# Two attention-and-MLP layers on one core: the last two chunks of a second product taken tile by tile, and four smaller moves of loads and steps around it

## The chip, the cores and the metric

The kernel runs on one core of one Trainium2 chip. The metric is the device time of one execution in microseconds (us). The kernel before was run three times: 2491.26, 2492.43 and 2493.83 us, median 2492.43. One more execution was profiled, and its records are the trace that is read here.

## The reference

The input is x of 2048 rows by D = 576 columns in f32. Two equal layers follow one another, each an attention and an MLP on a normalised x, with a residual sum after each:

```python
x = x + _A_ref(_layernorm(x), A_wqkv, A_w_phi, A_wo)      # twice in turn
x = x + _B_ref(_layernorm(x), B_w1, B_b1, B_w2, B_b2)

# _A_ref: 32 heads of width 18
q, k, v = split(x @ wqkv)
phi(t)  = concat(softmax(t @ w_phi), softmax(-(t @ w_phi)))
o       = phi(q) @ (phi(k)^T v) / (phi(q) @ sum(phi(k)) + 1e-6)
return o @ wo

# _B_ref: F = 4608
return relu(x @ w1 + b1)**2 @ w2 + b2
```

The attention is linear: the sums `phi(k)^T v` of all 2048 rows must be there before the first row of `o`, so each layer has a point at which every block waits for every other one.

## The kernel before

The rows lie in four blocks of 512 (`TB`), each of four tiles of 128 rows (`NT`); F lies in 36 chunks of 128 (`NF`). Operands of the products are split into a high and a low part, and each product is three matrix products (high by high, high by low, low by high). TensorE (PE) works through one fixed list of 15108 matmuls; VectorE (DVE), ScalarE (ACT) and GpSimd (POOL) normalise, split and add, and nearly all DMAs are issued from SyncE's queue (SP), in the order in which the program wrote them. No engine changes the order of its own list, so an instruction that waits holds up all that stands behind it on its engine.

The program is written with Python generators: `weave`, `lagged`, `pipeline`, `chained` and `paced` set by a table of costs in which order the steps of two generators are written, and `tc.issue_after(ins)` makes what stands under it come behind `ins` in the written order.

The stages of a layer, with the names of tiles that the trace shows (`a_2`, `m_3` and so on are block numbers; layer 0 takes the blocks in the order 3, 2, 0, 1, layer 1 in the order 1, 0, 3, 2):

- A barrier finishes the keys of the last block and then runs the attention's output stage for the first block (`g_out` with `pause`, L895 on). Tiles there begin with `t0` in layer 0 and `t1` in layer 1: `t0fQ2e` and `t0fQ3e` are the exponentials of the queries of row tiles 2 and 3, `t0opt` their transposes, `t0oo0h`/`t0oo1l` the two halves of wo in high and low parts, stored to memory as `wsoh`/`wsol` for later blocks, `t0ox` the rows of x, `t0opo` the product with wo, `t0onn`/`t0onp`/`t0onh` the normalised rows, their transposes and these in high part.
- `g_mlp` does the MLP of the first block (`m_3` in layer 0), woven with the attention of the second (`a_2`), and then that of the second block (`m_2`), woven with the attention of the two last (`a_0`, `a_1`). For each chunk `first` loads w1 (`r1`) and w2 (`r2`, L1093) and splits them (ACT takes the high part of w2 at L1100 as `m_2s`), `hidden` is the first product, `square` the activation, and `second` the second product. The first two chunks' `hidden` are done in halves of 256 columns, the second half after the last transposes of the normalised rows (`last`, L1065 to L1074, called through `rest` at L1164).
- `g_pair` does the MLP of the two last blocks together (tiles `m_p...`). `products` forms the first product of both by a Strassen-like scheme and the second product of the one block; `seconds` forms the second product of the other, chunks 36 to 71, with row sums in the PSUM tiles `m_pach` and `m_pacacc`; `last_rows` (L1478 to L1499) ends each of the two: the last chunk, four transposes back (`m_ppy<-ident,m_pyt`), the sum with the residual rows `m_px` (the first 448 columns, `:R`, at L1496 and the last 128 at L1492), and the stores.
- In layer 0 the `seconds` are woven at a rate of 0.85 with `back_keys`: the norms, keys and values of layer 1 for three blocks (tiles `n_3`, `w_3v`, `k_0K3`). Its norm is `g_norm` with `fine` (L542): `begin` takes the statistics of a row tile (`n_3s`, `n_3m`) and the factor `n_3d`, which POOL forms; `scale` writes `n_3n` and `n_3e`; transposes (`n_3p`) and splits (`n_3h`, `n_3l`) follow. After the `seconds` come the values and keys of the last block, with a norm of its own (`n_last`).

Around the change, these lists of the program set the order: in `g_out`, `pieces()` loads or forms the halves of wo and `keep_split` stores them; `between` holds twelve small steps between the two parts of the paused block; in the main loop `next(back)` sets how many steps of `back_keys` are written before the `seconds` begin.

Of the kernel before, what the change touches and what calls it, by code (L numbers as in the profile page):

```python
# [15 lines left out]
NT = TB // P  # L16
# [5 lines left out]
def layers_kernel(  # L22
# [18 lines left out]
    nc = tc.nc  # L41
# [410 lines left out]
    def g_norm(x_of, dst, name, then=None, fine=False):  # L452
# [86 lines left out]
            else:  # L539
                split_main(i // 3 * 2 + i % 3, pts.pop(i))  # L540

        yield from pipeline(NT, (start, apart), (2.0, 1.6))  # L542
        yield from pipeline(3 * NT // 2, (cross, split), (0.3, 0.9))

    def spill(b, x):
# [312 lines left out]
    def g_out(layer, b, ph, dst, name, parts=1, pause=None, behind=None, norm=None, mid=None, costs=(None, None)):  # L858
# [88 lines left out]
        if pause:  # L947
            product, total, factors, rescale = pause()
            with tc.issue_after(dense["scaled0"].ins):
                product(2, 0)  # L950
                total(2, 0)
        pair = pieces() if behind or "o" in kept else None
        if pair:
            keep_split("o", pair)
        if pause and not late:
            late_products()
        xs_of = []
        yield

        def between(pts):  # L960
            steps = [lambda: product(3, 0), lambda: total(2, 1), lambda: factors(2), lambda: rescale(2, 1),
                     lambda: total(3, 0), lambda: total(3, 1), lambda: factors(3), lambda: rescale(3, 1),
                     lambda: o_add(xs_of[0], pts[0], 0), lambda: o_add(xs_of[1], pts[1], 0),
                     lambda: rescale(2, 0), lambda: rescale(3, 0)]
            for step in steps:
                step()
                yield

        for part in range(parts):
            if pause and part:  # L970
                xs_of += [rows_in(t) for t in range(2)]
                pts = [o_product(t, half) for half in range(2) for t in range(2)]
                with tc.issue_after(dense["part"].ins):
                    drain(chained(between(pts), every=True))
            for i, _ in enumerate(lagged(2 * NG, lambda i: turn(part, i), lambda i, f: times(part, i, f), parts)):
                if pause and part and i in (1, 2):
                    with tc.issue_after(dense["turned"].ins):
                        o_add(xs_of[i - 1], pts[1 + i], 1)
                yield costs[0]
# [84 lines left out]

        def last():  # L1065
            spare.update(tags=[f"acc{i}" for i in range(NC)], i=NC + 1)
            pts = [main[0](t, xns[t]) for t in (2, 3)]
            pts.append(rest[0](1))
            spare["tags"] = []
            yield  # L1070
            main[1](2, pts[0])
            main[1](3, pts[1])
            rest[1](1, pts[2])
            yield  # L1074

        dense["rest"] = last()
# [2 lines left out]
    def g_mlp(layer, b, x, after, name, rest=None, then=None):  # L1079
# [277 lines left out]
    def g_pair(layer, blocks, x, after, name):  # L1357
# [119 lines left out]

        def last_rows(b):  # L1478
            f = (b + 1) * NF - 1
            features(f, range(3))  # L1480
            yt = sb.tile([P, TB], F32, tag="hr", name=f"{name}yt{b}", bufs=2)
            nc.scalar.activation(yt, accs[b][KC], AF.Copy)
            by_rows(f, range(2), range(3))
            pt = ps_w.tile([P, TB], F32, tag="w", name=f"{name}py{b}")
            p3 = pt.rearrange("p (t d) -> p t d", d=P)
            for t in range(NT):
                nc.tensor.transpose(p3[:, t], yt[:, t * P : (t + 1) * P], ident)
            xs_ = after if b else []
            for t in range(NT):
                xr = sb.tile([P, D], F32, tag="x", name=f"{name}x{b}{t}", bufs=5)  # L1490
                nc.sync.dma_start(xr, xm[blocks[b]][t])
                nc.vector.tensor_add(xr[:, R:], p3[:, t], xr[:, R:])  # L1492
                xs_.append(xr)
            by_rows(f, range(2, NT), range(3))
            for t, xr in enumerate(xs_):
                dense["added"] = nc.vector.tensor_add(xr[:, :R], accs[b][t][:, :R], xr[:, :R])  # L1496
                at = blocks[b] * TB + t * P
                nc.sync.dma_start(out[at : at + P] if layer else xs[blocks[b]][t], xr)
            del high[f], wide[f]  # L1499

        def keep_high(f, r):
            nc.scalar.activation(r, r, AF.Relu)
# [78 lines left out]
        def seconds():  # L1581
            accs[1] = [ps_a.tile([P, TB], F32, tag=tag, name=f"{name}ac{tag}") for tag in ("h", "acc0", "acc1", "acc2", "acc3")]
            for f in range(NF, NF + 3):
                load_wide(f)
                load_high(f)
            for f in range(NF, 2 * NF - 1):
                if f + 3 < 2 * NF:
                    load_wide(f + 3)
                    load_high(f + 3)
                for t in range(NT):  # L1590
                    by_rows(f, [t], range(3))
                    yield
                features(f, range(3))
                del high[f], wide[f]
                yield
# [125 lines left out]
    for layer in range(2):  # L1721
# [145 lines left out]
```

## Time and profile before

| | |
|---|---|
| runs, us | 2491.26, 2492.43, 2493.83; median 2492.43 |
| profiled execution, its own time, us | 2491.15 |
| span of its records, us | 2489.2 |
| TensorE, busy and share of the span | 2463.1 us, 99% |
| VectorE | 1535.0 us, 62% |
| ScalarE | 1263.0 us, 51% |
| GpSimd | 956.7 us, 38% |
| granted TensorE clock, mean of the span | 0.999 |

Times in the rows of the trace are microseconds from the start of the span: first the start, then the busy time, then the engine (SPq is the queue that SyncE issues from), the line, the operation, the tile written and the tiles read, and a count where several equal rows stand in one. In square brackets stands how long the engine was idle just before, and what ended that. The view of waits has the engine, tile and line that waited, what released it, and then the sum in us, the count and the longest one.

### The profile page before, as it was taken

How to read it: one execution, taken by the hardware profiler on the slowest of the kernel's cores; microseconds unless marked ns; L12 is line 12 of the kernel's file. 1: busy time of each engine (PE TensorE's matmuls, PEld its weight loads, DVE VectorE, ACT ScalarE, POOL GpSimd, SP SyncE). 2: the span in 40 equal slices, each digit the busy share in tenths (PEclk: the TensorE clock that was granted, in tenths of full speed). 3: DMA queues.
4: the chain of work that ended last, by engine and by line, in shares of the span. 5: the costliest groups of instructions: out<-in, count | busy, mean ns of one | idle time of the engine just before them, and what ended most of it. 6: DMA issues, size and time to landing. Idle time of an engine off the chain costs nothing. (4 is left out here: it accounts for less than half of the span.)

```text
span 2489.2 us, 41471 instructions
## 1 busy us (share of the span) xinstructions
PE 2463.1 (99%) x15108; PEld 2169.4 (87%) x15108; DVE 1535.0 (62%) x2507; ACT 1263.0 (51%) x2243; POOL 956.7 (38%) x1101
## 2 busy tenths in 40 slices
PE   8999999999999999999999999999999999999999
PEld 8998888889888888888999988888888888888888
DVE  7778938454756655545756787584557665454454
ACT  4344545443546766664443445554445466666543
POOL 4445303212335565541433442132122355565322
PEclk9999999999999999999999999999999999999999
DMA  9124533346434433338754144334473444333363
GB/s 332 60 71 146 169 105 94 103 156 224 131 120 134 146 104 105 110 100 287 250 196 144 54 169 116 103 99 117 153 243 96 125 136 139 115 104 112 108 200 127
DMA packets 248892, 348.67 MB, mean 140 GB/s; under 512 B 30127, under 2 KB 155951, under 8 KB 246127
## 3 DMA queue, kind: packets, MB, share of 16 engines
q1 hardware_dynamic: 247428, 344.66, 44.0%
q8 instruction: 118, 1.93, 0.3%
q10 hardware_dynamic: 1258, 1.37, 0.2%
q14 instruction: 88, 0.71, 0.1%
HBM read 280.93 MB, written 65.00 MB: 139 GB/s over the span
## 5 line engine op out<-in xcount | busy, mean ns | idle before, releaser
L1428 POOL TENSOR_TENSOR m_ps<-m_pr,m_ps 128x128 fp32r<-128x128 f32 x144 | 118.2, 821 | 310.9 <-ACT m_ps L1426 248.7
L1427 DVE TENSOR_TENSOR m_ps<-m_pr,m_ps 128x448 fp32r<-128x448 f32 x144 | 97.9, 680 | 166.1 <-ACT m_ps L1426 162.6
L1470 PE MATMUL m_pacc<-m_ps,m_phb 128*128 128x448 f32 x864 | 188.5, 366 | 0.0
L1470 PEld LDWEIGHTS m_pacc<-m_ps,m_phb 128*128 128x128 f32 x864 | 162.1, 188 | 18.2
L1426 ACT ACTIVATE m_ps<-m_pr 128x576 fp32r<-128x576 f32 x144 | 98.4, 683 | 128.1 <-issue 71.5
L1470 PE MATMUL m_pacacc<-m_ps,m_phc 128*128 128x448 f32 x648 | 150.3, 368 | 0.7 <-DVE m_px L1496 0.7
L1470 PEld LDWEIGHTS m_pacacc<-m_ps,m_phc 128*128 128x128 f32 x648 | 119.2, 188 | 10.0 <-DVE m_px L1496 1.0
L1148 PE MATMUL m_0acc<-m_0s,m_0hb 128*128 128x448 f32 x432 | 100.2, 366 | 0.0
L1148 PE MATMUL m_2acc<-m_2s,m_2hb 128*128 128x448 f32 x432 | 100.2, 366 | 0.0
L1148 PE MATMUL m_3acc<-m_3s,m_3hb 128*128 128x448 f32 x432 | 99.7, 365 | 0.0
L1148 PE MATMUL m_1acc<-m_1s,m_1hb 128*128 128x448 f32 x432 | 99.7, 365 | 0.0
L1121 PE MATMUL m_3ph<-t0onh,m_3h 128*128 128x512 f32 (+1 forms) x380 | 97.6, 382 | 0.6 <-ACT t0onh L488 0.5
L1121 PE MATMUL m_1ph<-t1onh,m_1h 128*128 128x512 f32 (+1 forms) x380 | 97.5, 382 | 0.6 <-ACT t1onh L488 0.5
L1121 PE MATMUL m_2ph<-a_2nh,m_2h 128*128 128x512 f32 (+1 forms) x380 | 97.7, 384 | 0.0
L1121 PE MATMUL m_0ph<-a_0nh,m_0h 128*128 128x512 f32 (+1 forms) x380 | 97.6, 384 | 0.0
L1148 PEld LDWEIGHTS m_2acc<-m_2s,m_2hb 128*128 128x128 f32 x432 | 80.9, 188 | 10.6 <-ACT m_2hb L1129 0.2
L1148 PEld LDWEIGHTS m_0acc<-m_0s,m_0hb 128*128 128x128 f32 x432 | 80.9, 188 | 10.6 <-ACT m_0hb L1129 0.2
L1148 PEld LDWEIGHTS m_1acc<-m_1s,m_1hb 128*128 128x128 f32 x432 | 81.1, 188 | 10.3
L1148 PEld LDWEIGHTS m_3acc<-m_3s,m_3hb 128*128 128x128 f32 x432 | 81.1, 188 | 10.3
L1106 POOL TENSOR_TENSOR m_3s<-m_3r,m_3s 128x128 fp32r<-128x128 f32 x36 | 24.6, 684 | 161.6 <-ACT m_3s L1100 148.1
L1106 POOL TENSOR_TENSOR m_1s<-m_1r,m_1s 128x128 fp32r<-128x128 f32 x36 | 24.2, 673 | 162.2 <-ACT m_1s L1100 154.8
L1106 POOL TENSOR_TENSOR m_0s<-m_0r,m_0s 128x128 fp32r<-128x128 f32 x36 | 28.1, 779 | 138.8 <-ACT m_0s L1100 131.1
(2439 smaller groups left out, 7341.3 us busy)
## 6 DMA issues: line engine op xcount, KB each, us to landing
m_pr<-in_B_w SPq DMA_DIRECT2D x144, 288.0 KB
m_pr<-in_B_w SPq DMA_DIRECT2D x72, 256.0 KB
hd<-m_pu SPq DMA_DIRECT2D x72, 256.0 KB
m_pg<-hd SPq DMA_DIRECT2D x72, 256.0 KB
m_3r<-in_B_w SPq DMA_DIRECT2D x36, 288.0 KB
m_2r<-in_B_w SPq DMA_DIRECT2D x36, 288.0 KB
m_1r<-in_B_w SPq DMA_DIRECT2D x36, 288.0 KB
m_0r<-in_B_w SPq DMA_DIRECT2D x36, 288.0 KB
```

The lines of the kernel that those rows point to most:

```text
L1106: nc.gpsimd.tensor_sub(s2[:, D + R : 2 * D], r2[:, R:], s2[:, R:D].bitcast(F32))
L1121: dense["hidden"] = nc.tensor.matmul(ph[:, cols], a, m, start=(k == 0), stop=(k == len(ops) - 1))
L1148: nc.tensor.matmul(acc[t][:, :R], a[:, rows], m, start=(f == 0 and k == 0), stop=(f == NF - 1 and k == 2))
L1426: nc.scalar.activation(s2[:, :D], r2, AF.Copy)
L1427: nc.vector.tensor_sub(s2[:, D : D + R], r2[:, :R], s2[:, :R].bitcast(F32))
L1428: nc.gpsimd.tensor_sub(s2[:, D + R : 2 * D], r2[:, R:], s2[:, R:D].bitcast(F32))
L1470: nc.tensor.matmul(accs[b][t][:, :R], a[:, rows], m, start=(g == 0 and k == 0), stop=(g == NF - 1 and k == 2))
```

## The change

The arithmetic, the tiles' sizes and the number of matmuls stay. Six places are written in another order:

1. `g_norm`, fine path: the statistics of row tile t+1 are written before the scaling of row tile t; before, `pipeline` wrote both steps in its own order.
2. `g_out`: the first two loads of x rows stand ahead of the stores of the split wo. In `between`, `product(3, 0)` goes from first to fourth. Blocks without `behind` load their halves of wo at turn `NG` of the loop, where they did so after it.
3. `last` and `g_mlp`: the transposes of row tile 2 and its splits are written after the first half chunk of `hidden`, those of row tile 3 and the rest after the second; before, all stood after the second.
4. `last_rows` of the second block (`b = 1`): chunks `NF - 2` and `NF - 1` are taken together. The last 128 columns' sums (`features`) of both come first, then rows 0 and 1 with both chunks each, the transposes, and rows 2 and 3. Each row's two sums and its store follow one another. `seconds` ends one chunk earlier.
5. `last_rows` of the first block (`b = 0`): all four sums of the 448 columns first, then for each row the sum of the 128 columns and its store.
6. Main loop: one step of `back_keys` is written before the last pair ends, and one after the `added` of `last_rows`, where there were two and four.

```diff
@@ g_norm
-        yield from pipeline(NT, (start, apart), (2.0, 1.6))
+        start(0)
+        yield 2.0
+        for t in range(NT):
+            if t + 1 < NT:
+                start(t + 1)
+                yield 2.0
+            apart(t)
+            yield 1.6
@@ g_out
-        pair = pieces() if behind or "o" in kept else None
-        if pair:
-            keep_split("o", pair)
+        pair = pieces() if behind else None
         if pause and not late:
             late_products()
         xs_of = []
+        if pause:
+            xs_of += [rows_in(t) for t in range(2)]
+            keep_split("o", pair)
         yield
...
-            steps = [lambda: product(3, 0), lambda: total(2, 1), lambda: factors(2), lambda: rescale(2, 1),
+            steps = [lambda: total(2, 1), lambda: factors(2), lambda: rescale(2, 1), lambda: product(3, 0),
...
-                xs_of += [rows_in(t) for t in range(2)]
...
+                if not behind and i == NG:
+                    pair = pieces()
@@ last
-            pts = [main[0](t, xns[t]) for t in (2, 3)]
-            pts.append(rest[0](1))
+            pt = main[0](2, xns[2])
             spare["tags"] = []
-            yield
-            main[1](2, pts[0])
-            main[1](3, pts[1])
-            rest[1](1, pts[2])
+            main[1](2, pt)
+            yield
+            spare.update(tags=[f"acc{i}" for i in range(NC)], i=NC + 2)
+            pt, pr = main[0](3, xns[3]), rest[0](1)
+            spare["tags"] = []
+            main[1](3, pt)
+            rest[1](1, pr)
             yield
@@ g_mlp
-        if rest:
-            with tc.issue_after(dense["hidden"].ins):
-                drain(rest)
+            if rest:
+                with tc.issue_after(dense["hidden"].ins):
+                    next(rest)
@@ g_pair, last_rows
-            features(f, range(3))
+            fs = (f - 1, f) if b else (f,)
+
+            def rows_of(ts):
+                for t in ts:
+                    for f in fs:
+                        by_rows(f, [t], range(3))
+
+            for f in fs:
+                features(f, range(3))
...
-            by_rows(f, range(2), range(3))
+            rows_of(range(2))
...
-                nc.vector.tensor_add(xr[:, R:], p3[:, t], xr[:, R:])
+                if b:
+                    nc.vector.tensor_add(xr[:, R:], p3[:, t], xr[:, R:])
                 xs_.append(xr)
-            by_rows(f, range(2, NT), range(3))
+            rows_of(range(2, NT))
             for t, xr in enumerate(xs_):
                 dense["added"] = nc.vector.tensor_add(xr[:, :R], accs[b][t][:, :R], xr[:, :R])
+            for t, xr in enumerate(xs_):
+                if not b:
+                    with tc.issue_after(dense["added"].ins):
+                        nc.vector.tensor_add(xr[:, R:], p3[:, t], xr[:, R:])
                 at = blocks[b] * TB + t * P
                 nc.sync.dma_start(out[at : at + P] if layer else xs[blocks[b]][t], xr)
...
-            for f in range(NF, 2 * NF - 1):
+            for f in range(NF, 2 * NF - 2):
@@ main loop
-                    for _ in range(2):
-                        next(back, None)
+                    next(back, None)
         with tc.issue_after(dense["added"].ins):
-            for _ in range(4):
-                next(back, None)
+            next(back, None)
         weave(seconds, back, 0.85)
```

Three places show how the instructions move on their engines. The numbers behind the names tell tiles of one name apart.

The first is SyncE's queue in layer 0 where the paused block stores its split wo. Before:

```order
L406 DMA wsol<-t0oo0l 126x1152
L406 DMA wsol<-t0oo0l 72x288
L406 DMA wsol<-t0oo1l 126x1152
L406 DMA wsol<-t0oo1l 72x288
L922 DMA t0ox_3119<-in_A_x 128x576
L922 DMA t0ox_3121<-in_A_x 128x576
```

And now:

```order
L406 DMA wsol<-t0oo0l 126x1152
L929 DMA t0ox_3006<-in_A_x 128x576
L929 DMA t0ox_3008<-in_A_x 128x576
L406 DMA wsol<-t0oo0l 72x288
L406 DMA wsol<-t0oo1l 126x1152
L406 DMA wsol<-t0oo1l 72x288
```

The two loads of x rows have passed three stores, two of them of the low half `t0oo1l`.

The second is SyncE's queue in layer 0 at the step from the MLP of block 3 to that of block 2. `a_0o1h` and `a_0o1l` are loads of wo's second half for block 0, `xs` the stores of block 3's rows, `m_2r_2` and `m_2r_3` the loads of w2 for chunks 2 and 3. Before:

```order
L987 DMA xm_3_96<-a_2x_5675 128x576
L406 DMA a_0o1h<-wsoh 126x1152
L406 DMA a_0o1h<-wsoh 72x288
L406 DMA a_0o1l<-wsol 126x1152
L1204 DMA xs_0_81<-m_3x_5979 128x576
L1204 DMA xs_1_82<-m_3x_5981 128x576
L1204 DMA xs_2_83<-m_3x_5983 128x576
L1204 DMA xs_3_84<-m_3x_5985 128x576
L406 DMA a_0o1l<-wsol 72x288
L1093 DMA m_2r_2_6197<-in_B_w 128x576
L1093 DMA m_2r_3_6211<-in_B_w 128x576
```

And now:

```order
L996 DMA xm_3_96<-a_2x_5675 128x576
L1104 DMA m_2r_2_6185<-in_B_w 128x576
L406 DMA a_0o1h<-wsoh 126x1152
L1215 DMA xs_0_81<-m_3x_5979 128x576
L1215 DMA xs_1_82<-m_3x_5981 128x576
L1215 DMA xs_2_83<-m_3x_5983 128x576
L1215 DMA xs_3_84<-m_3x_5985 128x576
L1104 DMA m_2r_3_6199<-in_B_w 128x576
L406 DMA a_0o1h<-wsoh 72x288
L406 DMA a_0o1l<-wsol 126x1152
L406 DMA a_0o1l<-wsol 72x288
```

The load `m_2r_2` stands ahead of the four row stores now, and the loads of `a_0o1` partly behind them. On the four compute engines nothing moves at this place, and the step in layer 1 moves alike.

The third is VectorE in layer 0 where `products` ends and `seconds` begins. `m_ps_36` and `m_phc` are the split operands of chunk 36, the first of the `seconds`. Before:

```order
L438 BN_STATS n_3s_11924<-x_3_0_11922 128x6 x2
L441 BN_AGGR n_3m_11925<-n_3s_11924 128x2
L469 TENSOR_SCALAR n_3n_11932<-x_3_0_11922,n_3m_11925,n_3d_11926 128x512
L470 TENSOR_SCALAR n_3e<-x_3_0_11922,n_3m_11925,n_3d_11926 128x128
L1496 TENSOR_TENSOR m_px_11951<-m_pacc_9173,m_px_11951 128x448
L1496 TENSOR_TENSOR m_px_11954<-m_pacc_9174,m_px_11954 128x448
L1492 TENSOR_TENSOR m_px_11951<-m_ppy_11946,m_px_11951 128x128
L1492 TENSOR_TENSOR m_px_11954<-m_ppy_11946,m_px_11954 128x128
L1492 TENSOR_TENSOR m_px_11957<-m_ppy_11946,m_px_11957 128x128
L1492 TENSOR_TENSOR m_px_11960<-m_ppy_11946,m_px_11960 128x128
L1496 TENSOR_TENSOR m_px_11957<-m_pacc_9175,m_px_11957 128x448
L1496 TENSOR_TENSOR m_px_11960<-m_pacc_9176,m_px_11960 128x448
```

And now:

```order
L438 BN_STATS n_3s_11924<-x_3_0_11922 128x6 x2
L441 BN_AGGR n_3m_11925<-n_3s_11924 128x2
L1438 TENSOR_TENSOR m_ps_36_11991<-m_pr_36_11989,m_ps_36_11991 128x448
L1540 TENSOR_TENSOR m_phc_11997<-m_pg_11995,m_phc_11997 128x512
L1516 TENSOR_TENSOR m_px_11948<-m_pacc_9173,m_px_11948 128x448
L1516 TENSOR_TENSOR m_px_11950<-m_pacc_9174,m_px_11950 128x448
L1516 TENSOR_TENSOR m_px_11952<-m_pacc_9175,m_px_11952 128x448
L1516 TENSOR_TENSOR m_px_11954<-m_pacc_9176,m_px_11954 128x448
L1520 TENSOR_TENSOR m_px_11948<-m_ppy_11943,m_px_11948 128x128
L1520 TENSOR_TENSOR m_px_11950<-m_ppy_11943,m_px_11950 128x128
L1520 TENSOR_TENSOR m_px_11952<-m_ppy_11943,m_px_11952 128x128
L1520 TENSOR_TENSOR m_px_11954<-m_ppy_11943,m_px_11954 128x128
```

The split of chunk 36 stood behind all of these rows and now stands ahead of the residual sums; the scaling of the first row tile (`n_3n`, `n_3e`) now comes after the operands of chunks 38, 40 and 41. On TensorE the transposes `n_3p` of that norm begin in chunk 39, where they began in chunk 37, and the three chunks before run without other work between.

More of the change, by code (lines that the diff above doesn't have):

```diff
@@ L1491, in last_rows @@
                 nc.sync.dma_start(xr, xm[blocks[b]][t])
-                nc.vector.tensor_add(xr[:, R:], p3[:, t], xr[:, R:])
+                if b:
+                    nc.vector.tensor_add(xr[:, R:], p3[:, t], xr[:, R:])
                 xs_.append(xr)
-            by_rows(f, range(2, NT), range(3))
+            rows_of(range(2, NT))
             for t, xr in enumerate(xs_):
                 dense["added"] = nc.vector.tensor_add(xr[:, :R], accs[b][t][:, :R], xr[:, :R])
+            for t, xr in enumerate(xs_):
+                if not b:
+                    with tc.issue_after(dense["added"].ins):
+                        nc.vector.tensor_add(xr[:, R:], p3[:, t], xr[:, R:])
                 at = blocks[b] * TB + t * P
                 nc.sync.dma_start(out[at : at + P] if layer else xs[blocks[b]][t], xr)
-            del high[f], wide[f]
+            for f in fs:
+                del high[f], wide[f]
         def keep_high(f, r):
```

## The prediction

> **What bounds the kernel now.** I read the page's busy times first, then the view of TensorE's (PE) waits, then the lists of rows around each wait that the change can reach.
>
> ```profile
> PE 2463.1 (99%) x15108; PEld 2169.4 (87%) x15108; DVE 1535.0 (62%) x2507; ACT 1263.0 (51%) x2243; POOL 956.7 (38%) x1101
> ```
>
> PE is busy for 99% of the span and the change leaves it the same 15108 matmuls, so all that can be won lies in PE's idle time, 2489.2 − 2463.1 = 26.1 us, part of which is the start before the first product and the end after the last. The waits within reach are few and single:
>
> ```profile
> PE t0opt L888 <- DVE t0fQ2e L805: 3.1, 1, 3.1
> ...
> PE n_3p L494 <- DVE n_3l L489: 1.9, 1, 1.9
> PE a_3pn L904 <- DVE a_3fl L891: 1.8, 1, 1.8
> ...
> PE a_0pn L904 <- DVE a_0fl L891: 1.2, 1, 1.2
> ...
> PE m_1ph L1121 <- ACT t1onh L488: 0.5, 1, 0.5
> PE m_3ph L1121 <- ACT t0onh L488: 0.5, 1, 0.5
> ```
>
> Each of these six occurs once, 9.0 us in all; two more, 1.52 together, stand in part C. Since PE's list is the bound, a microsecond of wait removed from it is worth up to a microsecond, and work on the other engines is free as long as PE does not wait for it. That is the rule by which I cost each part.
>
> **Part A: the x rows ahead of the stores of split wo (layer 0).**
>
> ```profile
> 204.20 1.05 SPq L406 DMA_DIRECT2D wsol<-t0oo0l  x2
> ...
> 207.67 3.96 POOL L384 TENSOR_TENSOR t0oo1l<-t0oo1r,t0oo1h 126x1152 fp32r<-126x1152 f32 x2
> ...
> 209.00 1.98 DVE L828 TENSOR_TENSOR t0fm<-t0fQ3e,zb 128x576 f32<-128x576 f32 x1
> ...
> 212.04 1.78 SPq L922 DMA_DIRECT2D t0ox<-in_A_x  x4
> ...
> 215.00 0.23 DVE L800 TENSOR_TENSOR t0fQ3r<-t0fQ3r,t0fu 128x64 f32<-128x64 f32 x1
> ...
> 216.16 0.46 DVE L939 TENSOR_TENSOR t0ox<-t0opo,t0ox 128x288 f32<-128x288 f32 x1 [0.94 <-DMA t0ox<-in_A_x]
> ...
> 218.09 0.75 DVE L805 TENSOR_TENSOR t0fQ2e<-t0fQ2e,t0fQ2r 128x576 f32<-128x576 f32 x1
> ...
> 218.98 0.41 PE L888 MATMUL t0opt<-ident,t0fQ2e 128*126 128x128 f32 x2 [3.07 <-DVE t0fQ2e L805]
> ```
>
> PE names VectorE (DVE) as what it waits for, but DVE itself stood idle for 0.94 us until a DMA landed. The load was issued at 212.04, because SyncE's queue (SP) held a store of `t0oo1l`, which GpSimd (POOL) finished at 207.67 + 3.96 = 211.63. The change puts two loads behind the first store of `t0oo0l`, so they are issued near 204.20 + 0.5 = 204.7. They landed 216.16 − 212.04 = 4.1 us after issue; now that is about 208.8. The sums then start when DVE's own chain ends, 215.00 + 0.23 = 215.2; two sums of 0.46 and the rescaling of 0.75 end at 216.9, and PE starts 218.98 − 218.84 = 0.14 later, near 217.05. Gain 218.98 − 217.05 = **1.9 us**. At most the whole 3.07 goes. At least 1.9 − 1.2 = 0.7 does: the product of 1.98 at 209.00 has 576 columns like the rescaling of 0.75 but ran beside POOL's 3.96 us, and the steps of DVE's chain now come in another order there, so that some other sum may be held up the same 1.2 us in its place or beside it. The Trainium skill (SBUF — State Buffer, SBUF: two separate sides) states that DVE sums with two operands in SBUF and GpSimd's instructions that read SBUF take one port pair by an exclusive lock for a whole instruction. The row at 209.00 agrees with it: 1.98 is just one of POOL's two subtractions (3.96/2); by the lock a second sum caught there would take up to 1.98 more, and part A would be about nothing.
>
> **Part B: w2 of chunk 2 ahead of the row stores (both layers).**
>
> ```profile
> 516.70 2.60 SPq L1204 DMA_DIRECT2D xs<-m_3x  x4
> ...
> 520.24 1.07 SPq L1093 DMA_DIRECT2D m_2r<-in_B_w  x2
> ...
> 524.17 0.40 PE L1139 MATMUL m_2acc<-m_2hb,m_2s 128*128 128x512 f32 x1
> ...
> 525.97 0.69 ACT L1100 ACTIVATE m_2s<-m_2r 128x576 fp32r<-128x576 f32 x1 [2.10 <-DMA m_2r<-in_B_w]
> 526.56 1.06 ACT L890 ACTIVATE a_0fh<-a_0pt 126x512 fp32r<-126x512 f32 x2
> ...
> 527.97 0.50 PE L904 MATMUL a_0pn<-a_0fh,kbh 126*126 126x512 f32 x1 [1.23 <-DVE a_0fl L891]
> ```
>
> The chain is again a DMA seen through two engines: the load is issued at 520.24, ScalarE (ACT) waits 2.10 us for it with `a_0fh` queued behind, DVE makes `a_0fl` from that, and PE starts 527.97 − 525.97 = 2.00 us after ACT did. PE would have been free at 527.97 − 1.23 = 526.74. Now the load goes ahead of the stores that began at 516.70, at least 3.5 us earlier. ACT's next limit is the buffer of `m_2s`, which chunk 0's second product leaves when its last matmul ends, 524.17 + 0.40 = 524.57. ACT then runs from 524.6, PE could start at 526.6, and that is before 526.74: the whole 1.23 goes.
>
> ```profile
> 1748.03 0.91 SPq L1093 DMA_DIRECT2D m_0r<-in_B_w  x2
> ...
> 1754.50 0.68 ACT L1100 ACTIVATE m_0s<-m_0r 128x576 fp32r<-128x576 f32 x1 [2.66 <-DMA m_0r<-in_B_w]
> ...
> 1756.49 0.50 PE L904 MATMUL a_3pn<-a_3fh,kbh 126*126 126x512 f32 x1 [1.79 <-DVE a_3fl L891]
> ```
>
> Layer 1 has the same shape: PE 1.99 us behind ACT, free at 1754.70; ACT needs to start at 1752.7, 1.8 us earlier than now, and it has been idle for 2.66. Gain **1.23 + 1.79 = 3.0 us**, bounds 0 (the load still late) and 3.0. What is delayed in turn are the loads of `a_0o1` behind the stores, by the four stores' 2.60 us and one load; they are wanted by the output product only after all of block 0's attention numerators, so I take nothing for them.
>
> **Part C: start of the seconds in layer 0.**
>
> ```profile
> 1139.60 2.41 SPq L1498 DMA_DIRECT2D xs<-m_px  x4
> ...
> 1140.75 0.47 PE L1470 MATMUL m_pacacc<-m_ps,m_phc 128*128 128x448 f32 x1 [0.67 <-DVE m_px L1496]
> ...
> 1142.41 1.13 SPq L1742 DMA_DIRECT2D x<-xs  x2
> ...
> 1142.87 0.47 PE L1470 MATMUL m_pach<-m_ps,m_phc 128*128 128x448 f32 x1 [0.85 <-DVE m_ps L1427]
> ...
> 1148.77 0.55 DVE L469 TENSOR_SCALAR n_3n<-x,n_3m,n_3d 128x512 f32<-128x512 f32 x1 [1.00 <-POOL n_3d L443]
> ...
> 1151.54 0.67 DVE L469 TENSOR_SCALAR n_3n<-x,n_3m,n_3d 128x512 f32<-128x512 f32 x1 [1.00 <-POOL n_3d L443]
> ...
> 1152.38 1.28 DVE L489 TENSOR_TENSOR n_3l<-n_3p,n_3h 128x512 fp32r<-128x512 f32 x2
> ...
> 1153.12 0.44 PE L494 MATMUL n_3p<-ident,n_3e 128*128 128x128 f32 x2 [1.90 <-DVE n_3l L489]
> ```
>
> In the queue of DVE before, the normalisation and all residual sums stood ahead of chunk 36's operands, so PE waited 0.67 and 0.85. Now chunk 36's split comes first and PE runs chunks 36 to 38 with nothing between: 1.52 go. The 1.90 at 1153.12 is a wait for `n_3l` behind DVE steps that twice stood idle 1.00 us for POOL's `n_3d` (ahead of 1148.77 and of 1151.54). With the next tile's statistics written first, most of those 2 × 1.00 is covered by the other work that the look-ahead puts there, and this wait shrinks; but the transposes now also come in a tighter group, with two PSUM tiles to turn over, and I leave 1.0 of it. Gain 1.52 + 0.90 = **2.4 us**; at most 0.67 + 0.85 + 1.90 = 3.42, at least 0 (all of it comes back as waits for the norm three chunks later).
>
> **Part D: the later start of the back work, end of layer 0.** Four steps fewer are written ahead of the seconds, so the chain of layer 1's keys ends later. Its last softmax meets this:
>
> ```profile
> 1344.28 0.62 DVE L1496 TENSOR_TENSOR m_px<-m_pach,m_px 128x448 f32<-128x448 f32 x1 [5.30 <-PE m_pach L1470]
> ...
> 1355.22 0.60 ACT L488 ACTIVATE n_lasth<-n_lastp 128x512 fp32r<-128x512 f32 x1 [0.88 <-PE n_lastp L480]
> ```
>
> DVE waits 5.30 us for PE there, and the next norm's split waits for PE too (0.88), not PE for it. Three chunks of a pace of 0.85 make the softmax some 5 us later, which that idle time takes up. Cost **0**; if the cover fails by 1 us, PE loses that 1 us at the next norm.
>
> **Part E: the end of the program.**
>
> ```profile
> 2483.68 1.99 SPq L1498 DMA_DIRECT2D out<-m_px  x4
> ...
> 2484.16 1.15 DVE L1496 TENSOR_TENSOR m_px<-m_pacacc,m_px 128x448 f32<-128x448 f32 x2
> ...
> 2484.50:2485.50 1.00, 0.00 (x0) 0.00 (x0) 0.81 (x2) 0.00 (x0) 0.00 (x0) 1.00 0.98 376
> ...
> 2487.50:2489.20 1.70, 0.00 (x0) 0.00 (x0) 0.00 (x0) 0.00 (x0) 0.00 (x0) 0.50 0.04 14
> ```
>
> The last sum ends at 2484.16 + 1.15 = 2485.3; the four stores (4 × 128 × 576 × 4 bytes = 1.18 MB) fill the DMA engines from 2484.5 at 376 GB/s, 3.1 us, to 2487.6. So the end is set by the stores' bytes after a late first issue. Now six matmuls of the chunk before stand behind rows 0 and 1 and the transposes; at 0.2 us each (2463.1 us for 15108 is 0.16, and these are wide ones) the first two stores go about 1.1 us ahead of 2483.68; the last row's sum still follows the last matmul and its store is issued near 2485.1. It starts 2484.5 − 2483.7 = 0.8 to 1.0 later and takes 0.78, to 2486.9. Gain **0.8 us**, bounds 0.2 and 1.2. The Trainium skill (DMA: Bandwidth & Descriptors, Anatomy of one DMA — SWDGE (gpsimd) path) fits a fixed 2.0 us beside the bytes of one transfer, on GpSimd's path; by that figure, an estimate for SyncE's, the last store would complete at 2485.1 + 2.0 + 0.78 = 2487.9 and this term would be about 0.2. The windows show the first bytes within a microsecond of the issue and little after 2487.6, so less than that here.
>
> **Part F: transposes between the half chunks (both layers).**
>
> ```profile
> 238.09 0.49 DVE L469 TENSOR_SCALAR t0onn<-t0ox,t0onm,t0ond 128x512 f32<-128x512 f32 x1
> ...
> 241.72 1.68 PE L1121 MATMUL m_3ph<-t0onh,m_3h 128*128 128x256 f32 x9 [0.52 <-ACT t0onh L488]
> ```
>
> The wait of 0.52 is for the splits of tiles 2 and 3 done at once; with tile 2 earlier it shrinks to some 0.3. But tile 2's transposes now stand half a chunk earlier, at about 238.2, and its scaling on DVE ends at 238.58: 0.4 of new wait. Loss **0.2 us** in each layer, 0.4 in all, bounds a loss of 1.0 and a gain of 0.3.
>
> **Sum.** 1.9 + 3.0 + 2.4 + 0 + 0.8 − 0.4 = 7.7 us. The profiled execution took 2491.15 by its own time, so 2483.45; the median of the runs is 2492.43 − 2491.15 = 1.28 above it, so I forecast **2484.7 us**. About 0.2% (5 us) is what a measurement of this kernel can tell from no change.
>
> **Rivals.**
> 1. *Part C comes back as waits.* The norm's transposes are denser and its rows are loaded behind the four stores. For it: only two PSUM tiles turn over; against: the two idle stretches of 1.00 vanish. Then the sum is 7.7 − 2.4 = 5.3, or less with a new wait of 2: 2487.1 to 2489.
> 2. *Part B doesn't come.* The margin is thin, 526.74 − 526.6 = 0.14 us, and if the landing rather than the buffer still ends ACT's wait, the 3.0 stay. For it: SP is backed up at both places; against: 3.5 us of lead for 1.4 needed. The sum is 4.7: 2487.7, within 0.2%.
> 3. *Slower: x rows late at the start of the seconds.* `x_3_1` to `x_3_3` were issued partly before and now all behind the stores of 1139.60, near 1142.8. DVE stands in order, so a late row stops the operands of later chunks too, and PE with them. At part A's 4.1 us from issue to landing they come at about 1147; by its list DVE comes to the first of them after the residual sums and six splits for chunks 38 to 41, whose operands wait on PE's pace, at about 1147 to 1148. Each microsecond beyond costs PE up to one; it decides when the landing slips by more than 7.7 us, past 1155. With 4 us more than that, 2496.4. For it: the in-order queue; against: a slip twice the usual latency.
> 4. *The edits move waits but remove none*: PE stays at the same total because each place hands its wait on to the next in-order queue (A to DVE's lock, B to ACT's buffer, C to the norm); only E remains, 2491.6.
>
> **How the numbers follow.** Forecast 0.60, rival 1 0.14, rival 2 0.10, rival 3 0.09, rival 4 0.07. The likeliest case's own range is 2482.0 to 2487.0 (A 0.7 to 3.07, C 1.5 to 3.42, E and F by their bounds, not all at one end). With rivals 1, 2 and 4 the range is 2481.0 to 2491.5, which leaves out rival 3 and some of the tails. Faster by over 0.2% (below 2487.4): the forecast 0.60 and a little of rivals 1 and 2, 0.64. Slower: 0.09, rounded to 0.10. Within: the rest, 0.26.
>
> **What would show it.** A: no DMA as what ended DVE's idle time before `t0ox`, and PE's wait for `t0fQ2e` near 1. B: no wait at `a_0pn` and `a_3pn`, the load of `m_2r` no longer behind `xs`. C: no wait of PE at the first three chunks of the seconds, 1.0 or less at the later `n_3p`. E: last bytes about 2.4 us after the last matmul rather than 3.2. F: a wait of about 0.4 at tile 2's `t0onp`. The forecast is wrong if PE shows a new single wait over 2 us in layer 0's seconds or at `n_last`, or if the DVE chain ahead of `t0fQ2e` ends later than 215.2 by more than a microsecond.

## The result, and the profile after

The changed kernel takes 2487.36 us (median of 12 runs, 2483.86 to 2490.75), the kernel before 2491.66 in twelve runs beside it (2488.80 to 2495.03). The ratio is 0.9981 with a 95% interval of 0.9973 to 0.9989: 0.19% faster, or 4.7 us of 2491.7 with 2.7 to 6.7 as bounds. The forecast was 2484.7. The execution that was profiled took 2485.37, so it is one of the faster ones.

The page and the view of TensorE's waits of the changed kernel:

```profile
span 2483.7 us, 41469 instructions
PE 2463.2 (99%) x15108; PEld 2169.5 (87%) x15108; DVE 1533.9 (62%) x2507; ACT 1262.1 (51%) x2243; POOL 959.3 (39%) x1101
```

```profile
PE n_3p L480 <- DVE n_3n L469: 2.7, 1, 2.7
...
PE t0opt L895 <- DVE t0fQ2e L812: 1.2, 1, 1.2
...
PE m_1ph L1132 <- ACT t1onh L488: 0.5, 1, 0.5
PE m_3ph L1132 <- ACT t0onh L488: 0.5, 1, 0.5
```

The waits `a_0pn` (1.2) and `a_3pn` (1.8) are gone, `t0opt` fell from 3.1 to 1.2, and one new wait of 2.7 stands at `n_3p`, at the start of the seconds. To see what each place is worth, each matmul's start in one trace was set against the start of the same matmul in the other; the median difference over a quiet stretch behind each place gives the lead over the kernel before there. The steps of that lead in the two profiled executions are:

| place | forecast gain, us | lead gained, us |
|---|---|---|
| A, x rows ahead of the stores of wo | 1.9 | 2.9 |
| F, transposes between half chunks, both layers | −0.4 | −0.3 and −0.1 |
| B, w2 ahead of the row stores, layer 0 / layer 1 | 1.2 / 1.8 | 1.3 / 1.9 |
| C, start of the seconds (with D) | 2.4 | −1.2 |
| E, end of the program | 0.8 | 0.8 |
| sum | 7.7 | 5.3 |

The spans differ by 5.5 us (2489.2 against 2483.7); small drifts between the places make up the rest. One warning on such sums: over the first 190 us, where none of the kernels below differs, the profiled executions took from 0.9 us less to 1.9 us more than that of the kernel before, so in what follows a place is always read against the lead just ahead of it.

### The profile page after: what moved, and what is told of

It reads as the page before. It is cut to its first block, busy times and chain, and to the rows that moved or that the text cites. A ratio compares the mean times of both kernels' runs of the same rounds, so it can differ in the third digit from the quotient of the medians.

```text
span 2483.7 us, 41469 instructions
## 1 busy us (share of the span) xinstructions
PE 2463.2 (99%) x15108; PEld 2169.5 (87%) x15108; DVE 1533.9 (62%) x2507; ACT 1262.1 (51%) x2243; POOL 959.3 (39%) x1101
## 4 chain that ended last, share of the span: by engine, by line
PE 94%; DVE 3%; DMA 1%; ACT 1%; issue 1%; POOL 0%; SPq 0%; ACTq 0%; DVEq 0%; POOLq 0%
PE m_ppx L1449 9%; PE m_pacc L1481 7%; PE m_pacacc L1481 5%; PE m_ppy L1449 5%; PE m_1ph L1132 5%; PE m_3ph L1132 5%; PE m_0ph L1132 5%; PE m_2ph L1132 5%; PE m_2acc L1159 4%; PE m_0acc L1159 4%; PE m_1acc L1159 3%; PE m_3acc L1159 3%; PE m_ppz L1449 2%; PE m_pacc L1471 2%; PE m_pacacc L1471 2%; PE m_pach L1481 2%
## 5 line engine op out<-in xcount | busy, mean ns | idle before, releaser
L1132 PEld LDWEIGHTS m_3ph<-t0onh,m_3h 128*128 128x128 f32 x380 | 68.8, 188 | 14.0 <-ACT t0onh L488 0.7
```

The costliest lines, as they stand in the source:

```text
L1132: dense["hidden"] = nc.tensor.matmul(ph[:, cols], a, m, start=(k == 0), stop=(k == len(ops) - 1))
```

## The experiments

Profiles show single places to about 0.1 us, timed runs show totals to about 2.5 us; both are given. Ratios are to the kernel before on the same chip.

### Is the new wait a matter of buffers, of a backlog, or of the look-ahead?

The timeline of the changed kernel at the new wait (start, busy time, engine, line, operation, tiles; idle time and its releaser in brackets):

```profile
1136.33 2.88 SPq L1522 DMA_DIRECT2D xs<-m_px  x4
1143.72 1.71 SPq L1767 DMA_DIRECT2D x<-xs  x3
...
1143.60 0.68 DVE L1540 TENSOR_TENSOR m_phc<-m_pg,m_phc 128x512 fp32r<-128x512 f32 x1
1146.59 0.82 DVE L438 BATCH_NORM_STATS2 n_3s<-x 128x6 f32<-128x288 f32 x2 [2.32 <-DMA x<-xs]
...
1148.12 1.12 PE L480 MATMUL n_3p<-ident,n_3n 128*128 128x128 f32 x4 [2.67 <-DVE n_3n L469]
```

VectorE was through with the operands of chunk 41 at 1144.3 and then waited 2.32 us for a row of x, with the scaling of the first tile behind it, and TensorE behind that. The row's load was issued only at 1143.72, 4.5 us after the fourth store. SyncE had been waiting until 1143.68 for the first residual store to land: five buffers hold rows of x, and with the look-ahead the first row is still in use, so the second needs the buffer of a residual row. That store had been issued at 1136.33 and took 7.3 us; in the kernel before the x load that stood behind the same store went 2.8 us after its issue (1139.60 to 1142.41). Most of the bytes were through earlier than that, as the DMA share and GB/s at the end of these two rows show (1.01 and 371, then 0.39 and 153):

```profile
1136.00:1140.00 4.00, 4.00 (x21) 3.62 (x20) 2.03 (x7) 0.73 (x2) 0.47 (x1) 1.00 1.01 371
1140.00:1144.00 4.00, 4.00 (x21) 3.60 (x21) 2.63 (x4) 2.30 (x4) 1.58 (x2) 1.00 0.39 153
```

The last section shows what the store's landing still lacked.

**Six buffers**, wherever the rows' tag stands:

```diff
-                x = sb.tile([P, D], F32, tag="x", name=f"x1_{b}_{t}", bufs=5)
+                x = sb.tile([P, D], F32, tag="x", name=f"x1_{b}_{t}", bufs=6)
```

> The changed kernel with six instead of five buffers for rows of x. Ring theory: the 2.67 us wait of TensorE at the first n_3p (1148.12) exists because the load of x_3_1 needs the buffer of a residual row until that row's store has landed (SyncE waits for xs<-m_px until 1143.68). With a sixth buffer the load is issued right behind the four stores near 1139.3, the wait falls to 0.5 or less, the granted clock stays 1.00 to 1152, and from 1350 on the program is 6.0 to 6.6 us ahead of the kernel before (now 2.8): a time about 3.5 us shorter than the changed kernel's. Backlog theory: the DMA engines are full with w_3v and the stores until about 1142.5, so the load lands no earlier than 1146 anyway and the wait stays above 2 us. Look-ahead theory: VectorE scales the first tile only behind the second's statistics, and the wait stays near 2.7 whatever the buffers.

Measured: 2484.20 us, ratio 0.9974 (0.9964 to 0.9984). The wait did not go. `x_3_1` was now loaded early, and the third row took its place:

```profile
1139.70 4.10 SPq L1767 DMA_DIRECT2D x<-xs  x2
...
1146.28 0.82 DVE L438 BATCH_NORM_STATS2 n_3s<-x 128x6 f32<-128x288 f32 x2 [2.22 <-DMA x<-xs]
```

Issued at 1139.7, that row landed at 1146.2, 6.5 us later; TensorE waited 2.43 us at the second `n_3p` and 2.0 us for a key weight at 1191.4. So the ring of buffers is where the queue showed, and not the cause: the ring theory falls as it was stated, and the backlog theory's "lands no earlier than 1146" holds. (The wait for `x_3_1` itself went, which is the ring's part.) The place lost 1.9 us against the kernel before, 0.7 more than in the changed kernel; the intervals of the two kernels' timed ratios overlap.

**The old order of the norm.** `pipeline(NT, (start, apart), ...)` back in `g_norm`:

> The changed kernel with the norm's old order of steps (a tile's statistics, then its scaling, before the next tile's). Ring theory: the first tile is scaled at about 1144.9, so TensorE does not wait at the first n_3p (0.3 or less), but x_3_1 still lands late and its factor takes 1.0 us on GpSimd, so a wait of 1.5 to 2.5 appears at the second n_3p; end of layer 0 about 4 us ahead of the kernel before. Look-ahead theory: no wait above 0.5 at any n_3p, 6.5 us ahead. Backlog theory: as the ring theory.

Measured: one run, 2487.55. Waits of 2.40 at the second `n_3p` and 1.79 at the last transposes' (L494), and 1.54 for a key weight; the place cost 1.6 us against the kernel before. The look-ahead is not what makes the wait.

**All of part C undone**, also the order of sums and the counts of back steps:

> The changed kernel without look-ahead, with the old order of sums for the first block of the pair and with the old two and four steps of back work ahead of the seconds; the rest of the change stays. All theories: the four other parts keep their gains (2.9, 1.3, 1.8 and 0.8 less 0.3), the waits 0.67, 0.85 and 1.90 of the kernel before return around 1140 to 1153, and the program is 4.0 us ahead at 1350 where the changed one is 2.8 ahead: span about 6.7 us below the kernel before's, 1.2 below the changed kernel's.

Measured: 2485.25, ratio 0.9974 (0.9966 to 0.9983), 6.5 us by the ratio, as expected by the sum (6.7). The profile's lead was only 5.0 us net of the start, with the old waits at 0.67, 0.85 and 1.08; what it lost there is the subject of the clock below.

**The weights behind the rows.** What had come ahead of the stores on SyncE's queue were the loads of `w_3v`, 720 KB each. This edit orders them behind the loads of the x rows:

```diff
-                nc.sync.dma_start(x, xs[b][t])
+                dense["row"] = nc.sync.dma_start(x, xs[b][t])
...
-                        next(loads, None)
+                        with tc.issue_after(dense["row"].ins) if i == 0 else nullcontext():
+                            next(loads, None)
```

> The changed kernel, with the four loads of layer 1's value weights (w_3v, 720 KB each) issued behind the loads of the next x rows instead of ahead of the four residual stores. After the sixth buffer moved the wait from the first to the second tile and left it at 2.43 us, the theory is backlog: the stores and the x rows queue on the DMA engines behind 2.2 MB of w_3v, so a row takes 6.6 us from issue to landing. Without it the stores land by about 1140, x_3_1 is issued by 1140 and lands by 1143.5, TensorE's wait at n_3p falls from 2.67 to 0.5 or less, there is no half clock there, and the end of layer 0 is 6 to 7 us ahead of the kernel before (changed: 2.8); time about 3.5 us below the changed kernel's. If the wait stays above 2 us, backlog is not the cause either and the look-ahead order itself is.

> The same late weights with six buffers for rows of x as well. Backlog theory: as with five, n_3p's waits 0.5 or less, since the ring costs nothing once stores land in 3 us; within 0.5 us of the run with late weights alone at the end of layer 0. Ring theory: the sixth buffer brings 1 us or more beside it.

Measured: 2481.14, ratio 0.9961 (0.9948 to 0.9975), and with six buffers 2483.06, ratio 0.9964 (0.9952 to 0.9977). The timeline with five:

```profile
1139.48 2.21 SPq L1522 DMA_DIRECT2D xs<-m_px  x4
1144.12 1.75 SPq L1767 DMA_DIRECT2D x<-xs  x3
1145.92 0.42 SPq L406 DMA_DIRECT2D w_3v0h<-wsvh  x1
...
1148.94 0.65 PE L480 MATMUL n_3p<-ident,n_3n 128*128 128x128 f32 x4 [0.78 <-DVE n_3n L469]
```

The store takes 4.6 us to land in place of 7.3, the wait is 0.78 us (1.27 with six buffers, at the second tile), and the place gains 1.8 and 2.2 us against the kernel before: what the prediction's term of 2.4 had meant. The waits missed the expected 0.5, the stores did not land by 1140 as expected, and five buffers and six are equal within what can be told. Over all profiles the landing goes with the order of the weights: the first of the four stores lands 6.1 to 7.3 us after its issue in the six that hold the weights ahead of it (whatever the buffers and the look-ahead), and 4.4 to 5.3 us after it in the four that hold them behind.

**The weights behind the rows, without look-ahead:**

> Late w_3v with five buffers and the norm's old order of steps. If look-ahead is worth what the prediction said (it covers GpSimd's 1.0 us per tile), waits at the later n_3p grow by 1 us or more in all against the run with late weights alone, and part C gains less than that run's 1.8. If the order of the weights is all that matters, part C gains 1.8 or more without it.

Measured: 2484.37, ratio 0.9973 (0.9961 to 0.9984).

```profile
1146.58 0.66 PE L480 MATMUL n_3p<-ident,n_3n 128*128 128x128 f32 x4 [1.51 <-DVE n_3n L469]
1153.65 0.41 PE L494 MATMUL n_3p<-ident,n_3e 128*128 128x128 f32 x2 [2.08 <-DVE n_3l L489]
```

The two waits are 3.6 us together, where the same place had 0.78 and 0.36 with look-ahead, and a half-clock stretch (next section) came behind the second. The place lost 0.2 us where it had gained 1.8. So the look-ahead does its work once the rows come in time.

### The clock behind a wait

Part A gained a full microsecond more than it took off the wait (2.9 against 3.07 − 1.24 = 1.83). The view by windows of both kernels shows why; its columns are the busy time of TensorE, of its weight loads, of VectorE, ScalarE and GpSimd, then the granted clock, the DMA share and GB/s. Kernel before:

```profile
216.92:220.33 3.41, 1.18 (x7) 0.74 (x7) 1.79 (x3) 0.40 (x2) 0.00 (x0) 1.00 0.39 150
220.33:223.74 3.41, 3.38 (x16) 3.38 (x16) 2.57 (x8) 2.39 (x7) 1.46 (x1) 0.50 0.00 0
```

Changed kernel, at the new wait:

```profile
1144.38:1147.79 3.41, 1.07 (x6) 0.59 (x4) 1.16 (x4) 0.00 (x0) 0.05 (x1) 1.00 0.88 268
1147.79:1151.20 3.41, 3.08 (x11) 2.76 (x12) 2.87 (x9) 1.25 (x2) 1.89 (x4) 0.50 0.98 295
1151.20:1154.61 3.41, 3.41 (x19) 3.10 (x18) 2.84 (x8) 2.33 (x5) 2.30 (x4) 1.00 1.01 379
```

In each, a stretch of 3.41 us in which TensorE was busy for about a third is followed by one of 3.41 us at half clock, in which it does half the work. In these two executions part A's edit took one such stretch away, and part C's wait brought one back. To test it on the kernel before, one product of wo (15 matmuls) was done twice inside the wait:

```diff
+                again = pts[3]
...
+                        nc.tensor.matmul(again[:, :HP], a, m[:w, g], start=(g == 0 and k == 0),
+                                         stop=(g == NG - 1 and k == 2))
```

> The kernel before with one product of wo (15 matmuls of 288 columns, 1.9 us) done twice in the stretch in which TensorE waits 3.07 us for t0fQ2e; nothing else moves. Clock theory: the wait of over 2.7 us lets the granted clock fall to 0.50 (220.8 to 223.3), which costs about 1.1 us beside the wait; with 1.9 us of work in the stretch the wait is 1.2, the clock stays 1.00, t0fQ2e's transposes still start at 219.0 and from 225 on the program is 0.9 to 1.2 us ahead of the kernel before. Rival: the slow stretch comes from the small transposes and what they wait for, not from the idle time before; then the clock still falls and the program is level (0 to 0.2).

Measured in the profile: the wait is 1.26 us, the clock is 1.00 throughout, and the program gains 0.9 us over the stretch, as the clock theory had it, though more matmuls were done. The timed runs, however, went the other way: 2494.78, ratio 1.0012 (1.0003 to 1.0022), a loss of 0.7 to 5.5 us. Part of that is the edit's own: it stands in code that both layers run, so the program has 15138 matmuls, 30 more and not 15. In layer 1 TensorE had waited only 0.44 us at this place, and the second product there loses 0.9 us of lead, which is all that layer 0 had won. The rest of the loss is not explained, and one profile cannot say how often the clock holds.

How often it falls, the other profiles tell. Without part C's edits it fell twice, at waits of 1.22 and of 0.67 with 0.85:

```profile
217.50:220.91 3.41, 1.99 (x15) 1.31 (x13) 2.57 (x5) 0.94 (x3) 0.74 (x1) 1.00 0.31 116
220.91:224.32 3.41, 3.41 (x18) 3.41 (x17) 2.34 (x7) 2.39 (x6) 2.04 (x2) 0.50 0.00 0
1139.10:1142.51 3.41, 1.95 (x7) 1.20 (x8) 3.05 (x7) 0.57 (x2) 1.00 (x2) 1.00 0.98 374
1142.51:1145.92 3.41, 3.41 (x11) 2.87 (x10) 2.24 (x5) 0.63 (x1) 0.57 (x1) 0.50 0.91 242
```

and with the old order of the norm it did not fall at a wait of 2.40:

```profile
1146.20:1149.60 3.40, 1.49 (x8) 1.01 (x6) 1.14 (x4) 0.85 (x2) 0.79 (x2) 1.00 0.95 290
1149.60:1153.00 3.40, 2.91 (x16) 2.66 (x17) 2.40 (x7) 1.48 (x3) 1.10 (x3) 1.00 0.94 325
```

Part A's edit, in eleven profiles that hold it whole, gained 2.9 to 3.0 us in eight, and 1.9 to 2.0 in the three in which a half-clock stretch fell behind its remaining wait of 1.2. All of these are counted from the one profile of the kernel before, in which the stretch did fall; how often it falls there is not known.

### Parts A, B, E and F alone

**Only the early rows (A)**, with the twelve steps between the parts in their old order:

> The kernel before with only the first two x rows loaded ahead of the stores of split wo; the twelve steps between the parts keep their order. If the late rows alone made TensorE's wait of 3.07 at t0fQ2e, it falls to 1.2 as in the changed kernel, and the program gains 1.8 us there, or about 2.9 where the half clock goes too. Rival: the order of the steps mattered as well; then the wait stays at 1.9 or more.

```profile
PE t0opt L888 <- DVE t0fQ2e L805: 1.4, 1, 1.4
```

The loads alone take 1.7 of the 1.8 us off the wait; the order of the steps gave 0.15. One run, 2489.91; a half-clock stretch fell here, so the place gained 1.7 us in all.

**The loads of wo's halves (B).** First they were put behind the loop:

> The changed kernel with wo's halves for blocks without `behind` loaded after the loop, as before. If the load of m_2r behind the row stores is the cause of part B, the waits at a_0pn and a_3pn return at 1.2 and 1.8 us, and the two steps gain nothing (0.2 us or less each) where the changed kernel gained 1.3 and 1.8. Rival: another of the edits removed them; then they stay away.

The waits stayed away, and the two steps gained 1.3 and 1.9 as before. The undo was at fault: the section on the change above says that the kernel before loads these halves after the loop, and that is wrong. It has `pair = pieces() if behind or "o" in kept` ahead of the loop, so for these blocks the change moves the loads later. With that line back:

> The changed kernel with wo's halves for blocks without `behind` loaded at the start of the block, which is where the kernel before really has them (the earlier run put them behind the loop, later than either). The queue of SyncE at this step then has the old order again, m_2r behind four row stores. If that is the cause of part B, the waits at a_0pn and a_3pn return at 1.2 and 1.8 us and the two steps gain 0.2 or less. If they stay away, the cause is elsewhere.

```profile
PE a_3pn L911 <- DVE a_3fl L898: 3.0, 1, 3.0
...
PE a_0pn L911 <- DVE a_0fl L898: 1.3, 1, 1.3
```

Both waits are back (one run, 2494.65), the one in layer 1 longer than before and with a half-clock stretch behind it: that step lost 2.8 us. So B's cause is the queue, as predicted. The other reason for the long time of this run is part C, which cost it 4.0 us, with waits of 1.95, 1.49 and 1.6 and a half-clock stretch at 1193.3; with the same edits of part C it cost 1.2 in the changed kernel, 0.5 in the run with these loads behind the loop and 0.7 in the run with part E undone.

**Only the last chunk tile by tile (E undone):**

> The changed kernel with only the last chunk of the pair's second block done tile by tile at its end, as before. The stretch from the last matmul's end to the end of the span was 0.83 us shorter in the changed kernel than before; undone, it is as before (4.7 us, 0.1 less at most). If it stays shorter, another edit did it.

From the last matmul's end to the end of the span 4.73 us, in the kernel before 4.73, in the changed one 3.90. One run, 2485.97.

**Part F undone**, on top of late weights and six buffers:

> The run with late w_3v and six buffers, and with the transposes of row tiles 2 and 3 back behind both half chunks as in the kernel before (part F undone). If part F costs what the traces show (0.3 us in layer 0, 0.06 in layer 1), the two stretches cost nothing against the kernel before and the program ends 0.3 to 0.4 us earlier for it; the rest as in the run with six buffers: waits at n_3p of 1.3 or less, part A 1.9 or 2.9 by whether a half-rate window falls there. Time 2480 to 2483, below both given kernels.

Measured: 2483.04, ratio 0.9965 (0.9953 to 0.9977). The two stretches cost nothing (0.03 us or less), where they cost 0.25 and 0.1 us in the same kernel with part F. That gain is below what timed runs can tell. This run and the two with late weights are the fastest tried, 8.7 to 9.7 us below the kernel before by their ratios; among the three no order can be given.

## Why the prediction was right, and where it was not

The direction, the range (2481.0 to 2491.5) and five of the six parts held. The likeliest case's own range, 2482.0 to 2487.0, was missed by 0.4 us, and the gain of 0.19% stays just short of the 0.2% that had 0.64 of the chance beyond it. By the prediction's own sign its forecast failed in part C: a new single wait of over 2 us in layer 0's seconds was to show that, and there is one of 2.67. The time of 2487.36 lies in rival 1's 2487.1 to 2489 (part C comes back as waits, chance 0.14), which names the rows loaded behind the four stores among its reasons. That the total came within 2.7 us of the forecast owes something to luck: in the profiles part C came out 3.6 us under its term, and part A 1.0 us over its own by a clock that the sum did not have in it.

**A** came by the predicted chain:

```profile
204.66 1.29 SPq L929 DMA_DIRECT2D t0ox<-in_A_x  x2
...
215.05 0.81 DVE L946 TENSOR_TENSOR t0ox<-t0opo,t0ox 128x288 f32<-128x288 f32 x2
...
215.78 1.27 DVE L812 TENSOR_TENSOR t0fQ2e<-t0fQ2e,t0fQ2r 128x576 f32<-128x576 f32 x1
...
217.20 0.41 PE L895 MATMUL t0opt<-ident,t0fQ2e 128*126 128x128 f32 x2 [1.24 <-DVE t0fQ2e L812]
```

The loads went at 204.66 (204.7 was said), no DMA ended VectorE's wait, and TensorE started at 217.20 (217.05 was said). The rescaling took 1.27 us, not 0.75, beside a product of GpSimd's of 1.17 us that began at 215.27; with the lock that the Trainium skill describes (SBUF — State Buffer, SBUF: two separate sides) this agrees in direction. It is 0.5 us, not the 1.98 feared, and no run tested whether the lock is its cause. The term was too small by 1.0 us because the half clock behind a long wait was not in it.

**B** came as said, to 0.1 us in each layer:

```profile
511.18 0.36 SPq L1104 DMA_DIRECT2D m_2r<-in_B_w  x1
...
514.15 2.13 SPq L1215 DMA_DIRECT2D xs<-m_3x  x4
...
522.14 0.69 ACT L1111 ACTIVATE m_2s<-m_2r 128x576 fp32r<-128x576 f32 x1 [0.81 <-issue]
...
524.14 0.50 PE L911 MATMUL a_0pn<-a_0fh,kbh 126*126 126x512 f32 x1
```

No DMA ends ScalarE's wait any more, and TensorE starts 2.00 us behind it with no wait of its own.

**C** is the step that failed: 2.4 of gain forecast, 1.2 of loss measured. The first half was right: TensorE runs chunks 36 to 38 without the 0.67 and 0.85. Rival 3 named the right transfer and the right price, up to one microsecond of TensorE for each by which the row is late, but dated the row too early and got a small chance. To set its dates, which are those of the old trace, against the new one, 4.0 us must be taken off, the lead that A and B had gained by then. VectorE was to come to the row at 1147 to 1148; it was there at 1144.3, which is 1148.3 in the old dates, about as forecast. The row's load was to be issued at 1142.8; it went at 1143.72, 1147.8 in the old dates, 5 us later, since no thought was given to whose buffer it needs and to when the store from that buffer lands. It then landed after 2.9 us, not 4.1, and VectorE waited 2.32. And the look-ahead, priced only as a gain, puts that row's statistics ahead of the first tile's scaling, so that one late row stops the first transposes. Under this lies what the experiments showed: the 720 KB weight loads had moved ahead of the stores, which then took 7.3 us to land, where the prediction had the stores cost the time of their instructions only. With the weights behind the rows the part gains 1.8 to 2.2.

**D** held: no wait at the end of layer 0. **E** held to 0.1:

```profile
2477.76 3.01 SPq L1522 DMA_DIRECT2D out<-m_px  x4
...
2481.00:2482.00 1.00, 0.00 (x0) 0.00 (x0) 0.00 (x0) 0.00 (x0) 0.00 (x0) 1.00 0.71 281
2482.00:2483.70 1.70, 0.00 (x0) 0.00 (x0) 0.00 (x0) 0.00 (x0) 0.00 (x0) 0.62 0.02 8
```

The fourth store is issued at 2480.4, hardly a byte starts after 2482, and SyncE's wait for it ends at 2482.57, 2.1 us after the issue. The first of the four goes 2.0 us ahead of the last matmul's end (2479.75), where it went 0.8 us ahead of it before.

**F** cost 0.3 us in layer 0 and 0.1 in layer 1, where 0.2 in each was said:

```profile
235.74 0.66 PE L480 MATMUL t0onp<-ident,t0onn 128*128 128x128 f32 x4 [0.18 <-DVE t0onn L469]
...
239.20 0.97 PE L1132 MATMUL m_3ph<-t0onh,m_3h 128*128 128x256 f32 x6 [0.47 <-ACT t0onh L488]
```

Tile 2's transposes waited 0.18, not 0.4, and the wait that was to shrink to 0.3 stayed at 0.47.

## What to carry to other kernels

Price a moved load by the transfers issued ahead of it and by when the buffer that it takes comes free, not by the place of its instruction alone; here 2.2 MB of weights issued in the 7.2 us ahead of four stores turned a gain of 2 us into a loss. Before dates of two traces are set side by side, take off the lead gained ahead of the place. And a wait of about a microsecond on TensorE can cost another one by the clock behind it (1.0 at part A; a step of 3.41 us at half clock can lose at most 1.7, an estimate), so shortening a long wait can pay more than its length.

## What the runs showed of the hardware that was not expected

The granted clock changed in steps of 3.413 us on a grid that runs on through the whole execution and starts at another phase in each. In the 14 profiles, start and end of the program left out, seven grid steps had TensorE busy for under 0.45 of the step, and five of them were followed by one at 0.50 of the clock; of 14 with 0.45 to 0.60, six; of 13 with 0.60 to 0.70, none. What decides within the first two groups is not shown. So the same wait of 1.2 us at part A costs a microsecond more in one execution than in the next. With none to two such steps in each profile, an estimate is that this moves runs of one and the same kernel by up to 2 to 3 us; how much of their spread of 6 to 7 it makes was not measured. The Trainium skill (TensorE: Matmul & The Clock Gate, Part 1: The HAM clock gate) has this window, 3413 ns and free-running, and the half rate behind an idle one; the runs agree, and add that a window need not be idle for it.

The trace reports the landing of each of these stores as 16 counts, and the wait for it ends with the last one. In the changed kernel 14 of the 16 counts for the first residual store had come by 1140.02, the 15th came at 1141.30 and the last at 1143.66, so the buffer was held 3.6 us for two counts, the last 2.4 of it for one. In the kernel before all 16 counts of the same store came between 1141.75 and 1142.39. So of the 4.5 us by which the landing grew (2.8 to 7.3), the first 14 counts make about 1 and the last two the rest. With the weights behind the rows the last count still came 1.3 to 2.2 us after the 15th. Why these counts lag was not tried.
